# A causal attention and expert-layer kernel, with a copy, a rewrite of each partial sum and unread products added to the last half batch

## The chip, the cores and the metric

One core of a Trainium2 chip runs the kernel. The metric is the device time of one launch in microseconds (us), the median of several runs; lower is better. The engines are TensorE (PE in the profile; its weight loads are PEld), VectorE (DVE), ScalarE (ACT), GpSimd (POOL) and SyncE (SP, which here only issues DMAs). PSUM is the accumulator memory that TensorE writes its products to; SBUF is the working memory.

## What is computed

Block-causal attention over 8 batches and 8 heads of 576 positions and 64 dimensions, and behind it two matrix products with a gate between them, on 4608 tokens of 512 dimensions (the attention's output) and 2048 hidden units:

```python
def _attn_ref(q, k, v) -> np.ndarray:
    B, H, S, D = q.shape
    block = 64
    scale = 1.0 / np.sqrt(D)
    scores = scale * np.matmul(q, k.transpose(0, 1, 3, 2))
    ...
    scores = np.where(mask, scores, -1000000000.0)
    scores = scores - np.max(scores, axis=-1, keepdims=True)
    attn = np.exp(scores)
    attn = attn / (np.sum(attn, axis=-1, keepdims=True) + 1e-09)
    return np.matmul(attn, v).astype(np.float32)

def _moe_ref(x, w_in, w_out) -> np.ndarray:
    h = x @ w_in
    sp = np.where(h > 20.0, h, np.log1p(np.exp(np.minimum(h, 20.0))))
    g = h * np.tanh(sp)
    return (g @ w_out).astype(np.float32)
```

All inputs and outputs are float32.

## The kernel before

**Numbers in two parts.** TensorE takes float16 operands. Each float32 operand is scaled and split into a float16 part and a float16 remainder ("h" and "l": `wi_h` and `wi_l` for the first weights, `wo_h` and `wo_l` for the second, the halves of `Gt` for the gated values). A product of two such operands is three products into one accumulator: high by high, high weights by low values, low weights by high values.

**Half batches.** A batch's 576 tokens are two half batches (`Tile`), of 384 and 192 tokens. For the last batch the second half is 192 tokens (n = 192); it is the last of 16, numbered `self.i` = 15. Each half batch goes through four methods: `turn` (transposes the attention's output by DMA), `m1` (first matrix product and the gate on ScalarE), `split` (the gated values in two parts, `Gt`, on ScalarE and VectorE) and `m2` (second matrix product, eviction and store).

**The second product, `m2`.** The output's 512 dimensions are four slices of 128. A half batch of 192 tokens puts two slices side by side into one accumulator, a PSUM bank of 512 columns of which it uses 384 (`K` = 2), so the last one uses two accumulators: `acc0` for slices 0 and 1, `acc1` for slices 2 and 3. For each slice TensorE runs over f, the 16 blocks of 128 hidden units, with three products each (line 1702): 48 products of 128 weights by 192 columns, all added into the slice's columns. Each call of `add` in that loop makes one operation of three products, and the list `after` names what it waits for; `chain` keeps the slice's operations in order. When both slices of an accumulator are summed, `evac` scales them into `ot` (line 1734 where VectorE does it, 1741 where ScalarE does), and a DMA stores it (line 1759).

**What sets the order.** Nothing is issued while the operations are described. Each `add` records an engine, an estimated duration, a function that emits the instructions, what it waits for, and which buffers it takes and frees (a `Ring` stands for a set of equal buffers: `ss_ring` for two score tiles of 1024 columns in PSUM, `acc_ring` for three accumulators). `Plan.order` plays all operations through a model of the engines, in which an engine that comes free takes the ready operation with the earliest due time, and issues them in the order of the best play. Due times are the tables in `DUE`. Each engine then runs its instructions strictly in the order that was issued, and waits only for semaphores.

**The end of the program.** After the last `m1` there is no attention left, so TensorE runs the last half batch's `m2` alone. ScalarE evicts, SyncE stores, VectorE and GpSimd have nothing left.

Of the kernel before, what the change touches and what calls it, by code (L numbers as in the profile page):

```python
# [16 lines left out]
ALU = mybir.AluOpType  # L17
# [3 lines left out]
P = 128  # L21
# [326 lines left out]
def attention_moe(  # L348
# [17 lines left out]
    nc = tc.nc  # L366
    B, DM, S = qT.shape
# [62 lines left out]
    PT = [const.tile([P, 2048], F16, name=f"PT{i}") for i in range(NPT)]  # L430
# [14 lines left out]
    wi_h = const.tile([P, NP, DFF], F16, name="wi_h")  # L445
    wi_l = const.tile([P, NP, DFF], F16, name="wi_l")
    wo_h = const.tile([P, NF, DM], F16, name="wo_h")
# [12 lines left out]
    pv = room(NPV, "pv", [P, 19])  # L460
# [18 lines left out]
    NSS, NACC = 2, 3  # L479
# [1039 lines left out]
    class Tile:  # L1519
# [165 lines left out]
        def m2(self):  # L1685

            n, fc = self.n, self.fc
            chain = None
            self.reads, self.evacs = [], []
            K = self.K  # L1690
            for o in range(0, NP, K):
                plan.part("tile", self.i, 18 + o)
                parts = []
                for k in range(K):
                    for f in range(NF):
                        slot = (self.i * NG + f // FG) % NSLOT

                        def prods(o=o + k, k=k, f=f, slot=slot, parts=parts):
                            pt = acc_[parts[0].slot % NACC][:, k * n : (k + 1) * n]
                            gh, gl = (Gt[:, slot, x, f % FG, 0:n] for x in range(2))  # L1700
                            for z, (w, g) in enumerate(((wo_h, gh), (wo_h, gl), (wo_l, gh))):
                                nc.tensor.matmul(  # L1702
                                    pt,
                                    lhsT=w[:, f, o * P : (o + 1) * P],
                                    rhs=g,
                                    start=k == 0 and f == 0 and z == 0,
                                    stop=f == NF - 1 and z == 2,
                                    skip_group_check=True,
                                )

                        begin = k == 0 and f == 0
                        after = [chain]
                        if o == 0 and k == 0 and f % FG == 0:
                            after = after + self.splits[f // FG]
                        if o == 0 and begin:
                            after = after + [last.get("m2")]
                        if self.first and f == 0:
                            after = after + w_done[1][o + k]
                        chain = add(
                            "pe", products([n] * 3), prods, after, [acc_ring] if begin else []  # L1720
                        )
                        parts.append(chain)
                        if o + k == NP - 1 and f % FG == FG - 1:
                            self.reads.append(chain)

                last["m2"] = chain
                fo = self.batch["fc2"]
                ev_ = self.evacs


                def evac(op, o=o, c=parts[0], e=o // K):
                    for k in range(K):
                        cols = slice(k * n, (k + 1) * n)
                        op(
                            ot[ev_[e].slot % 2][:, cols],
                            acc_[c.slot % NACC][:, cols],
                            fc[:, 1, o + k : o + k + 1],
                        )

                def evac_act(evac=evac):  # L1740
                    evac(lambda o, i, s: nc.scalar.activation(o, i, AF.Copy, scale=s))  # L1741

                ev = add(
                    "dve",
                    K * dve(n, True),
                    lambda evac=evac: evac(nc.vector.tensor_scalar_mul),
                    [chain, fo, last.get("out")],
                    [ot_ring],
                    [(acc_ring, parts[0])],
                    other=[("act", K * act(n, True), evac_act)],  # L1750
                    psum=True,
                )
                ev_.append(ev)
                last["out"] = ev
                t0 = self.b * S
                last["store"] = add(
                    "sp",
                    dma(P * K * n * 4),
                    lambda o=o, ev=ev: nc.sync.dma_start(
                        out=outT[o * P : (o + K) * P, t0 + self.q0 : t0 + self.q1].rearrange(  # L1760
                            "(k p) t -> p k t", p=P
                        ),
                        in_=ot[ev.slot % 2][:, 0 : K * n].rearrange("p (k t) -> p k t", k=K),
                    ),
                    [ev, last.get("store")],
                    free=[(ot_ring, ev)],
                )
# [53 lines left out]
        tiles_by[b, 1].split()  # L1821
    tiles_by[B - 1, 1].m2()

    ops = plan.order()
    with tc.manual_schedule():
        for o in ops:
# [45 lines left out]
```

## Time and profile before

| | before |
|---|---|
| median of three runs | 996.82 us (995.87 to 998.99) |
| span of the profiled execution, first to last instruction | 996.9 us |
| TensorE busy | 973.1 us (98%) |
| VectorE busy | 668.5 us (67%) |
| ScalarE busy | 663.4 us (67%) |
| GpSimd busy | 115.0 us (12%) |
| mean granted TensorE clock | 0.995 |

The profile is of one execution; the three timed runs are others. For the profiled execution there is no time but its span, and the span lies on the median. A row of the timeline is: start in us, duration in us, engine, line of the kernel, operation, what it writes and reads, shapes, number of instructions merged into the row, and in brackets how long the engine was idle before and what ended that. A row of a group is: line, engine, operation, shapes, count, busy us and mean ns of one, then the idle time before it. A row of a table by stretches of time is: from and to, length, then for PE, PEld, DVE, ACT and POOL the busy us with the number of instructions, then the granted TensorE clock, the busy share of the DMA engines and GB/s. Matmuls are pipelined: the next one starts before the modelled end of the last, so the distance between starts is what counts.

### The profile page before, as it was taken

What the parts mean: (1) busy time and instruction counts of PE and PEld (TensorE: products, weight loads), DVE (VectorE), ACT (ScalarE), POOL (GpSimd) and SP (SyncE); (2) the same over time, 40 slices, a digit from 0 to 9 for tenths busy, and PEclk for the clock granted to TensorE, in tenths of its full rate; (3) what the DMA queues carried; (4) which work ended last, traced back from release to release, by engine and by line L of the source; (5) the groups of instructions that cost most, each with busy time, mean ns of one, the idle gap of its engine ahead of it and who ended that gap; (6) DMA issues with size and microseconds to landing.
All of it is one profiled execution on the core that took longest, in us unless ns stands there. A gap on an engine that the chain in (4) does not pass through costs nothing.

```text
span 996.9 us, 25050 instructions
## 1 busy us (share of the span) xinstructions
PE 973.1 (98%) x10576; PEld 722.2 (72%) x10576; DVE 668.5 (67%) x1411; ACT 663.4 (67%) x1062; POOL 115.0 (12%) x166
## 2 busy tenths in 40 slices
PE   6999879999999999999999999999999999999998
PEld 5677557786777867777677866777677776876787
DVE  5999999779899687564798378965389636420210
ACT  3769987769768678656788678887668835432221
POOL 0011232011112002000120031010011000000000
PEclk9999979999999999999999999999999999999999
DMA  9863755796677745472668377873277333420000
GB/s 324 270 174 113 183 97 140 152 180 149 119 165 163 163 100 110 91 161 50 143 151 171 71 135 137 156 148 50 57 173 146 76 69 82 82 57 1 25 17 25
DMA packets 275505, 121.56 MB, mean 122 GB/s; under 512 B 221376, under 2 KB 261568, under 8 KB 275392
## 3 DMA queue, kind: packets, MB, share of 16 engines
q1 hardware_dynamic: 275392, 119.97, 55.4%
q8 instruction: 82, 1.34, 0.5%
q14 instruction: 31, 0.25, 0.1%
HBM read 56.10 MB, written 9.44 MB: 66 GB/s over the span
## 4 chain that ended last, share of the span: by engine, by line
PE 86%; DVE 9%; DMA 2%; issue 1%; ACT 1%; SPq 1%; ACTq 0%; DVEq 0%
PE acc L1702 37%; PE acc L1597 35%; PE u L1419 7%; PE ss L1217 6%; DVE Gt L600 1%; DVE wo_h L600 1%; DMA x<-xt 1%; DVE wo_l L691 1%; DMA wo_l<-in_w_in_dram 1%; DVE PT L1045 1%; PE u L1151 1%; DVE pv L1258 1%; DMA PT<-P 1%; DVE P L1342 0%; DVE wi_l L691 0%
## 5 line engine op out<-in xcount | busy, mean ns | idle before, releaser
L1597 PE MATMUL acc<-x,wi_h 128*128 128x192 f16 (+1 forms) x2048 | 394.8, 286 | 4.1 <-ACT Et L1626 2.7
L1702 PE MATMUL acc<-Gt,wo_h 128*128 128x192 f16 (+1 forms) x2048 | 386.1, 287 | 0.2 <-DVE Gt L1673 0.2
L1702 PE MATMUL acc<-Gt,wo_l 128*128 128x192 f16 (+1 forms) x1024 | 293.7, 287 | 0.0
L1597 PE MATMUL acc<-x,wi_l 128*128 128x192 f16 (+1 forms) x1024 | 293.0, 286 | 0.0
L1597 PEld LDWEIGHTS <-wi_h 128*128 128x128 f16 x2048 | 191.1, 98 | 86.0 <-issue 8.5
L1702 PEld LDWEIGHTS <-wo_h 128*128 128x128 f16 x2048 | 187.6, 98 | 50.2 <-issue 3.3
L1626 ACT ACTIVATE Et<-acc,bv 128x384 f32<-128x384 f32 x192 | 109.4, 579 | 118.1 <-PE acc L1597 116.7
L1292 ACT ACTIVATE pe<-ss,pv 128x192 f32<-128x192 f32 (+1 forms) x280 | 148.1, 606 | 12.8 <-DVE pv L1266 8.2
L1673 DVE SCALAR_TENSOR_TENSOR Gt<-Et,bv,Gt 128x1536 f16<-128x1536 f32 (+1 forms) x64 | 91.3, 1432 | 78.7 <-ACT Gt L1658 78.3
L1258 DVE TENSOR_REDUCE pv<-ss 128x2 f32<-128x384 f32 (+4 forms) x140 | 106.0, 789 | 41.8 <-PE ss L1229 41.5
L1702 PEld LDWEIGHTS <-wo_l 128*128 128x128 f16 x1024 | 100.4, 98 | 34.0 <-issue 1.1
L1597 PEld LDWEIGHTS <-wi_l 128*128 128x128 f16 x1024 | 100.2, 98 | 33.1
L1342 DVE TENSOR_TENSOR P<-pe,P 128x256 f16<-128x256 f32 (+1 forms) x168 | 110.8, 700 | 14.9 <-ACT P L1336 13.3
L1292 ACT ACT_TABLE_LOAD x59 | 75.7, 1283 | 12.5 <-DVE pv L1266 7.8
L1336 POOL CAST P<-pe 128x256 f16<-128x256 f32 (+3 forms) x81 | 60.3, 777 | 201.9 <-DMA PT<-P 79.2
L1626 ACT ACT_TABLE_LOAD x62 | 79.5, 1283 | 1.1
L1419 PEld LDWEIGHTS <-PT 128*128 128x128 f16 x2128 | 72.8, 98 | 5.1 <-issue 0.6
L1419 PE MATMUL u<-VH,PT 128*128 128x65 f16 x1344 | 74.3, 193 | 0.0
L1658 ACT ACTIVATE Gt<-Et,bv 128x768 f16<-128x768 f32 (+1 forms) x51 | 63.4, 1248 | 15.9 <-PE acc L1702 14.0
L1419 PE MATMUL u<-VO,PT 128*128 128x64 f16 x784 | 72.6, 193 | 0.0
L1741 ACT ACTIVATE ot<-acc,bv 128x192 f32<-128x192 f32 (+1 forms) x46 | 21.1, 487 | 66.8 <-PE acc L1702 52.9
L1217 PEld LDWEIGHTS <-QH 64*128 64x128 f16 x896 | 27.4, 95 | 28.7 <-issue 13.5
(126 smaller groups left out, 978.7 us busy)
## 6 DMA issues: line engine op xcount, KB each, us to landing
out_dram<-ot SPq DMA_DIRECT2D x48, 192.0 KB, 2.0
wo_l<-in_w_in_dram SPq DMA_DIRECT2D x8, 1024.0 KB, 7.3
Gt<-in_w_out_dram SPq DMA_DIRECT2D x16, 512.0 KB, 4.5
kl<-in_v_dram SPq DMA_DIRECT2D x28, 288.0 KB, 3.1
ql<-in_q_dram SPq DMA_DIRECT2D x28, 288.0 KB, 3.0
kl<-in_k_dram SPq DMA_DIRECT2D x28, 288.0 KB, 3.1
VL<-in_v_dram SPq DMA_DIRECT2D x28, 192.0 KB, 2.9
VL<-in_v_dram SPq DMA_DIRECT2D x28, 96.0 KB, 3.1
```

The lines of the kernel that those rows point to most:

```text
L1217: nc.tensor.matmul(ss[:, 512 * a + col : 512 * a + col + n], lhsT=m[q_][hs, at : at + P], rhs=m[k_][hs, key : key + n], start=first, stop= ...
L1258: nc.vector.reduce_max(out=mx[:, c], in_=ss[:, :, c0:c1], axis=mybir.AxisListType.X)
L1292: nc.scalar.activation(pe[ex[r].slot][:, cols], ss_[S0[r].slot % NSS][:, cols], AF.Exp, scale=esc, bias=mx[:, c, a : a + 1],)
L1336: op(out=h, in_=x)
L1342: nc.vector.tensor_sub(l, x, h)
L1419: nc.tensor.matmul(out, lhsT=p_, rhs=v_, start=first, stop=True, skip_group_check=True,)
L1597: nc.tensor.matmul(pt, lhsT=w[:, d, f * P : (f + 1) * P], rhs=x[:, d, :], start=k == 0 and d == 0 and z == 0, stop=d == NP - 1 and z == 2, ...
L1626: nc.scalar.activation(Et[:, (self.i * NG + g) % NE, j : j + K, 0:n], acc_[c.slot % NACC][:, 0 : K * n].rearrange("p (k n) -> p k n", k=K) ...
L1658: lambda g_hi=g_hi, ev=ev: nc.scalar.activation(g_hi, ev, AF.Copy, scale=self.s_g),
L1673: lambda g_hi=g_hi, g_lo=g_lo, ev=ev: nc.vector.scalar_tensor_tensor(out=g_lo, in0=ev, scalar=self.s_g, in1=g_hi, op0=ALU.mult, op1=ALU.su ...
L1702: nc.tensor.matmul(pt, lhsT=w[:, f, o * P : (o + 1) * P], rhs=g, start=k == 0 and f == 0 and z == 0, stop=f == NF - 1 and z == 2, skip_gro ...
L1741: evac(lambda o, i, s: nc.scalar.activation(o, i, AF.Copy, scale=s))
```

## The change

Two pieces are added; nothing is removed.

In `m2`, for the last half batch alone and after f = 7 of each of its four slices, two operations are put into the chain. ScalarE copies the slice's partial sum from PSUM to a buffer in SBUF (`pe[0]`, columns 512 to 703), and VectorE rewrites the partial sum as twice the copy less itself, the same value. The product of f = 8 waits for that.

Behind everything else, with a due time of 2000 (later than any other), one operation of TensorE and seven of other engines are described. TensorE's `columns` waits for two score tiles, and runs 16 products with 64 columns of weights each, into the lower and the upper half of the partitions in turn (8 of 512 columns, 8 of 128), and two full products of 512 columns. ScalarE, VectorE and GpSimd then copy and add tiles of 512 columns, one behind the other. No output depends on them.

```diff
                         parts.append(chain)
+                        if self.i == 2 * B - 1 and f == 7:
+
+                            def again(op, k=k, parts=parts):
+                                pt = acc_[parts[0].slot % NACC][:, k * n : (k + 1) * n]
+                                op(pe[0][:, 512 : 512 + n], pt)
+
+                            chain = add("act", 0.6, lambda again=again: again(nc.scalar.copy), [chain])
+                            chain = add(
+                                "dve",
+                                0.6,
+                                lambda again=again: again(
+                                    lambda t, pt: nc.vector.scalar_tensor_tensor(
+                                        out=pt,
+                                        in0=t,
+                                        scalar=2.0,
+                                        in1=pt,
+                                        op0=ALU.mult,
+                                        op1=ALU.subtract,
+                                    )
+                                ),
+                                [chain],
+                            )
                         if o + k == NP - 1 and f % FG == FG - 1:
                             self.reads.append(chain)
...
     tiles_by[B - 1, 1].m2()
+
+    plan.due = 2000.0
+    idle = [last["S"]] + [x for t in heads.values() for hl in t for x in hl]
+    both = [add("pe", (0.01, 0.0), lambda: None, idle, take=[ss_ring]) for _ in range(2)]
+
+    def columns():
+        for n in (512, 128):
+            for k in range(4):
+                for a in range(2):
+                    nc.tensor.matmul(
+                        ss_[both[0].slot % NSS][64 * a : 64 * a + 64, 512 * a : 512 * a + n],
+                        lhsT=wi_h[:, a, 64 * k : 64 * k + 64],
+                        rhs=wo_h[:, k, 0:n],
+                        start=True,
+                        stop=True,
+                        skip_group_check=True,
+                    )
+        for a in range(2):
+            nc.tensor.matmul(
+                ss_[both[1].slot % NSS][:, 512 * a : 512 * a + 512],
+                lhsT=wi_h[:, a, 0:P],
+                rhs=wo_h[:, 0, 0:512],
+                start=True,
+                stop=True,
+                skip_group_check=True,
+            )
+
+    C = add("pe", (2.6, 6000.0), columns, both)
+    one, two = (lambda: ss_[both[1].slot % NSS][:, 0:512]), (lambda: ss_[both[1].slot % NSS][:, 512:1024])
+    side, three = pe[0][:, 0:512], pe[1][:, 0:512]
+    steps = (
+        ("act", lambda: nc.scalar.copy(side, one())),
+        ("dve", lambda: nc.vector.tensor_add(two(), two(), side)),
+        ("act", lambda: nc.scalar.copy(one(), two())),
+        ("dve", lambda: nc.vector.tensor_add(three, side, two())),
+        ("pool", lambda: nc.gpsimd.tensor_add(three, side, three)),
+        ("pool", lambda: nc.gpsimd.tensor_sub(PT[0][:, 0:512], side, PT[1][:, 0:512])),
+        ("pool", lambda: nc.gpsimd.tensor_scalar_mul(three, side, pv[0][:, 0:1])),
+    )
+    for i, (eng, emit) in enumerate(steps):
+        C = add(eng, 2.0, emit, [C], free=[(ss_ring, x) for x in both] if i == len(steps) - 1 else [])
```

The order that the plan makes of it differs from the order before only from the last `m2` on. On TensorE, `columns` comes between f = 7 and f = 8 of the first slice. The end of it and the next product, with the semaphores that the rows wait for, in the changed program (before, the product of f = 8 followed that of f = 7 directly, and its first row had no wait):

```order
L1854 MATMUL ss0_131<-wo_h_106,wi_h_104 64x128
L1863 LDWEIGHTS wi_h_104
L1863 MATMUL ss1_132<-wo_h_106,wi_h_104 128x512
L1863 LDWEIGHTS wi_h_104
L1863 MATMUL ss1_132<-wo_h_106,wi_h_104 128x512
L1702 LDWEIGHTS wo_h_106
L1702 MATMUL acc0_134<-Gt_62,wo_h_106 128x192 [waits DVE_49]
```

Here 18 products stand between the two, and the matmul of f = 8 waits for VectorE while its weight load does not. In the other three slices f = 8 waits in the same way, with no other product in between.

ScalarE's end of the program in the changed kernel, from the last eviction that is not of the last half batch (`acc0` and `acc1` are the accumulators, `ss1` the second score tile, `pe0` the buffer in SBUF; `x2` marks two equal rows):

```order
L1763 ACTIVATE ot1_130<-acc2_136,bv1_115 128x384 [waits DMAHW7_49,PE_49]
L1727 COPY pe0_123<-acc0_134 128x192 [waits PE_49]
L1876 COPY pe0_123<-ss1_132 128x512 [waits PE_49]
L1727 COPY pe0_123<-acc0_134 128x192 [waits DVE_49,PE_49]
L1878 COPY ss1_132<-ss1_132 128x512 [waits DVE_49]
L1763 ACTIVATE ot0_129<-acc0_134,bv1_115 128x192 [waits DMAHW0_49,PE_49]
L1763 ACTIVATE ot0_129<-acc0_134,bv1_115 128x192
L1727 COPY pe0_123<-acc1_135 128x192 [waits DVE_49,PE_49] x2
L1763 ACTIVATE ot1_130<-acc1_135,bv1_115 128x192 [waits DMAHW1_49,PE_49]
```

Before, the three kinds of rows with line 1763 (then 1741) followed one another; the six copies are new, and the evictions have kept their order behind them.

VectorE's end in the changed kernel, from its last work on `Gt`, which was its last row before:

```order
L1673 SCALAR_TENSOR_TENSOR Gt_62<-Et_61,bv1_115,Gt_62 128x4x192 [waits DVE_49,Activation_49] x2
L1734 SCALAR_TENSOR_TENSOR acc0_134<-pe0_123,acc0_134 128x192 [waits Activation_49]
L1877 TENSOR_TENSOR ss1_132<-ss1_132,pe0_123 128x512 [waits Activation_49]
L1734 SCALAR_TENSOR_TENSOR acc0_134<-pe0_123,acc0_134 128x192 [waits Activation_49]
L1879 TENSOR_TENSOR pe1_124<-pe0_123,ss1_132 128x512 [waits Activation_49]
L1734 SCALAR_TENSOR_TENSOR acc1_135<-pe0_123,acc1_135 128x192 [waits Activation_49] x2
```

The four rewrites of the partial sums (line 1734) and two sums of 512 columns are new, and each waits for ScalarE. GpSimd gets an instruction that loads its library anew and three operations of 512 columns behind its last row. SyncE's rows are the same.

## The prediction

> **What bounds the kernel now.** I read the page's busy shares first, then its slices, then the end of the chain that ended last, then the last 20 us in order of time.
>
> ```profile
> span 996.9 us, 25050 instructions
> PE 973.1 (98%) x10576; PEld 722.2 (72%) x10576; DVE 668.5 (67%) x1411; ACT 663.4 (67%) x1062; POOL 115.0 (12%) x166
> PE   6999879999999999999999999999999999999998
> DVE  5999999779899687564798378965389636420210
> ACT  3769987769768678656788678887668835432221
> PEclk9999979999999999999999999999999999999999
> ...
> 973.15 12.60 PE acc L1702 x130
> 985.75 7.23 issue
> ```
>
> TensorE is busy 98% of the span, and nearly full in every slice but three of the first six. VectorE and ScalarE have little left to do in the last slices. The chain ends in products of line 1702, the second matrix product of the last half batch. (The "issue" of 7.23 us is TensorE's work as well: the wait of the last eviction, whose releaser was not recorded.) So the end of the program is TensorE's last product plus a fixed tail. The rows at both ends of the last half batch's second product are these:
>
> ```profile
> 976.89 0.33 PE L1702 MATMUL acc<-Gt,wo_h 128*128 128x192 f16 x2
> ...
> 984.73 0.25 PE L1702 MATMUL acc<-Gt,wo_l 128*128 128x192 f16 x1
> ...
> 985.01 0.42 ACT L1741 ACTIVATE ot<-acc,bv 128x192 f32<-128x192 f32 x1 [7.34 <-PE acc L1702]
> ...
> 992.65 0.25 PE L1702 MATMUL acc<-Gt,wo_l 128*128 128x192 f16 x1
> 992.98 0.73 ACT L1741 ACTIVATE ot<-acc,bv 128x192 f32<-128x192 f32 x2 [7.24 <-issue]
> 993.74 0.38 SPq L1759 DMA_DIRECT2D out_dram<-ot  x1
> ```
>
> There are 192 products (four output slices of 16 f of three). From 976.89 to 992.65 they start 191 steps apart, so one every 0.0825 us without a hole. What is put into this stretch and is not hidden moves the end by its own length; the tail behind 992.65 keeps its shape.
>
> **The change part by part.** First, the four round trips. In each output slice the product of f = 8 now waits for a VectorE pass over the partial sum, which waits for a ScalarE copy, which waits for the product of f = 7. All three are in series, and each of TensorE's later products stands behind the one that waits. Nothing else of the program is left to fill the hole: in the order of the changed program only the first hole has other products in it. The prices come from these rows.
>
> ```profile
> 955.10 0.94 ACT L1658 ACTIVATE Gt<-Et,bv 128x768 f16<-128x768 f32 x1
> 956.07 1.02 DVE L1673 SCALAR_TENSOR_TENSOR Gt<-Et,bv,Gt 128x768 f16<-128x768 f32 x1 [21.72 <-ACT Gt L1658]
> ...
> 140.32 1.80 DVE L1673 SCALAR_TENSOR_TENSOR Gt<-Et,bv,Gt 128x1536 f16<-128x1536 f32 x1
> 141.44 0.13 PEld L1702 LDWEIGHTS <-wo_h 128*128 128x128 f16 x2
> 142.17 0.48 PE L1702 MATMUL acc<-Gt,wo_h 128*128 128x384 f16 x1 [0.22 <-DVE Gt L1673]
> ...
> L674 ACT CAST wi_l<-acc 128x512 f16<-128x512 f32 x8 | 4.7, 588 | 2.9 <-PE acc L665 2.9
> L1741 ACT ACTIVATE ot<-acc,bv 128x384 f32<-128x384 f32 x20 | 11.6, 579 | 30.5 <-PE acc L1702 23.9 <-issue 6.6
> L1741 ACT ACTIVATE ot<-acc,bv 128x192 f32<-128x192 f32 x26 | 9.5, 416 | 36.3 <-PE acc L1702 29.0 <-issue 7.2
> L600 DVE SCALAR_TENSOR_TENSOR Gt<-Gt 128x512 int32<-128x512 int32 x32 | 20.9, 688 | 0.1
> L1734 DVE TENSOR_SCALAR ot<-acc,bv 128x192 f32<-128x192 f32 x6 | 2.2, 410 | 2.6 <-PE acc L1702 2.6
> L1483 DVE TENSOR_TENSOR tt<-u,dv 128x384 f32<-128x384 f32 x32 | 17.8, 557 | 2.0
> L1483 DVE TENSOR_TENSOR tt<-u,dv 128x256 f32<-128x256 f32 x32 | 13.6, 424 | 2.3
> ```
>
> - The last product before the hole takes 0.25 us from its start to its modelled end. ScalarE starts 0.03 us after that (984.73 + 0.25 = 984.98, and 985.01).
> - The copy of 128x192 out of PSUM is not in the trace. The eviction of the same tile on the same engine takes 416 ns, and 579 for twice the columns, so 0.85 ns a column; but it reads a scale for each partition. The plain cast of 512 columns takes 588 ns; less 320 x 0.85 that is 316. I take 0.32, the row nearest in kind; the bounds are 0.22 (588 x 192 / 512, nothing of it fixed) and 0.42.
> - ScalarE to VectorE: 955.10 + 0.94 = 956.04, and 956.07, so 0.03 us.
> - The VectorE pass reads SBUF and PSUM and writes PSUM; no such operation is in the trace. A two-input operation on PSUM takes 557 ns for 384 columns and 424 for 256, so 1.04 ns a column and 358 for 192. The same kind of instruction with a constant takes 688 ns for 512 columns, so 355 for 192 at that slope; the one-input pass over the same accumulator takes 410. I take 0.38, bounds 0.35 and 0.45.
> - VectorE to TensorE: 140.32 + 1.80 = 142.12, and 142.17, so 0.05 us. There the weights had been loaded ahead, at 141.44; here the load has no wait either and is hidden in the same way.
>
> Together 0.25 + 0.03 + 0.32 + 0.03 + 0.38 + 0.05 = 1.06 us from the start of the last product to the start of the next, where 0.08 stood: **+0.98 us a hole**. The bounds are 0.85 (0.22 and 0.35) and 1.28 (0.42, 0.45, and 0.08 for each of the three handoffs, as from 992.65 + 0.25 to 992.98). Three holes stay empty: **+2.94 us**, bounds 2.55 and 3.84.
>
> Second, the products that nobody reads. They are not on an idle engine: TensorE runs them, in the first hole: 8 of 512 columns and 8 of 128 with 64 columns of weights each, then two of 512 with 128. The waiting product stands behind all of them. The nearest rows are products that use half of the array's rows, two heads in turn:
>
> ```profile
> 787.77 0.25 PE L1702 MATMUL acc<-Gt,wo_l 128*128 128x192 f16 x1
> ...
> 787.94 0.55 PEld L1217 LDWEIGHTS <-QH 64*128 64x128 f16 x12 [0.16 <-issue]
> 787.95 0.42 PE L1217 MATMUL ss<-KH,QH 64*128 64x448 f16 x6
> 788.21 0.41 PE L1217 MATMUL ss<-KL,QH 64*128 64x448 f16 x6
> ...
> 788.95 0.38 PE L1217 MATMUL ss<-KL,QH 64*128 64x64 f16 x4
> 789.17 0.38 PE L1217 MATMUL ss<-KH,QL 64*128 64x64 f16 x4
> 789.48 0.34 PE L1702 MATMUL acc<-Gt,wo_h 128*128 128x192 f16 x2
> ```
>
> One group of six is, for each of two heads, 448 + 64 + 64 = 576 columns, and the next group starts 0.26 us later. At 0.0825 us for 192 columns, 576 columns are 0.25 us and 1152 are 0.50: the two halves ran side by side. Going into that mode cost 0.10 us (787.77 + 0.08 = 787.85, and 787.95) and coming back 0.09 (789.17 + 0.22 = 789.39, and 789.48). Twelve weight loads took 0.55 us, 46 ns each. If halves of the array's columns pair as halves of its rows do, the 8 of 512 take four times 0.22 = 0.88 us; the 8 of 128 are bound by their eight loads, 0.37 (their columns alone are 0.22); the two wide ones take 0.44; the two switches 0.19. That is 1.88 us, more than the 0.98 of the round trip beside it, so the first hole costs **+1.88 us**. Bounds: 1.54 (no switch, loads hidden) and, one at a time, 8 x 0.22 + 8 x 0.055 + 0.44 + 0.19 = 2.83.
>
> The Trainium skill's page "TensorEngine Tiling (Array Packing)", in "Restrictions and Gotchas", says that column tiling cannot be had with the fast weight load. With the page "TensorE: Matmul & The Clock Gate", section "LDWEIGHTS", a load of 64 columns would be 53 ns, an estimate, so the eight loads 0.43 in place of 0.37, and the sum 4.88. The trace has no load of 64 columns to set against it.
>
> Third, the sums on ScalarE, VectorE and GpSimd. ScalarE's copies of 512 columns (0.59 us by line 674) stand behind the first and behind the second of the four short copies, VectorE's sums of 512 (about 0.69) likewise, and there are 2 us of products (24 x 0.0825) or more between one round trip and the next operation that anything waits for. So they cost nothing. That cover would go if they took over 2 us each; then the rest would be added. GpSimd's library instruction and its three operations come after its last work:
>
> ```profile
> 829.34 1.12 POOL L1504 CAST xt<-tt 128x256 f16<-128x256 f32 x1 [8.72 <-DVE tt L1483]
> L1336 POOL CAST P<-pe 128x512 f16<-128x512 f32 x15 | 9.6, 643 | 0.0
> ```
>
> The library instruction has 155 us from 830.5 to do its work in; the trace has no price for it. The three operations begin about when the second rewriting is done, some 11 us before the end; three at 0.64, or at three times that with two inputs, take 2 to 6 us. Nothing waits for them but the end. No DMA is added or moved, and the last stores keep their places.
>
> The sum is 2.94 + 1.88 = **+4.82 us**. The span of the profiled execution is 996.9 us, and the median of the three runs 996.82 (995.87 to 998.99), the same within a tenth, so the span can be used as it stands: **1001.7 us**, +0.48%.
>
> **The rivals.**
>
> *The 64-column products run one after the other.* For it: the trace shows only halves by rows side by side, none by columns. Against it: two neighbours write different partitions and banks, as those halves did. It gives 2.94 + 2.83 = 5.77, so 1002.7. The Trainium skill's "TensorE: Matmul & The Clock Gate", section "Packing small matmuls", has three column tiles at 2.38 times the speed of one; that speaks for the pairs, and no run here shows it.
>
> *The added products are hidden.* Then the change is only the four round trips: 4 x 0.98 = 3.92, so 1000.8. It needs the 18 products to take under 0.98 us, while 1.32 us of columns alone stand against it.
>
> *The clock drops in the holes.*
>
> ```profile
> 115.80:119.20 3.40, 1.92 (x12) 1.17 (x12) 3.37 (x8) 2.36 (x4) 0.28 (x1) 1.00 1.03 282
> 133.20:136.60 3.40, 0.05 (x2) 0.00 (x0) 3.26 (x8) 2.74 (x4) 2.48 (x2) 0.92 1.03 99
> 136.60:140.00 3.40, 0.61 (x6) 0.29 (x7) 3.37 (x9) 3.15 (x3) 1.34 (x1) 0.50 0.27 60
> 141.45:146.00 4.55, 4.33 (x18) 2.09 (x16) 4.52 (x7) 4.10 (x7) 1.92 (x1) 0.50 0.69 161
> ```
>
> The clock (the column before the last two) stayed at 1.00 through a stretch in which TensorE worked 1.92 of 3.40 us, and went to 0.50 only after one of 0.05. With a hole of 1 us in every 4 the emptiest 3.4 us are about 70% full. If it dropped all the same for one such stretch, 3.4 us at half speed would add 1.7: 4.82 + 1.70 = 6.52, so 1003.4 or more.
>
> *Not slower.* The last rows above are also the one large loss in the span that a run may or may not have: from 141.45 to some 146.5 TensorE worked at a granted clock of 0.50. 5.1 us at half speed are 2.6 us lost. If the runs of the changed kernel that set its median met the clock back at 1.00 at 141.45 and those of before did not, 4.82 - 2.6 = 2.2 us remain: 999.1, within 0.3%. It decides from 1.8 us on (4.82 less the 3.0 us that are 0.3%). For it: the three runs lie 3.1 us apart. Against it: up to 977 us both programs have the same instructions in the same order.
>
> **How the numbers follow.** Forecast 0.57, one at a time 0.21, hidden 0.03, clock 0.05, not slower 0.14 (0.02 of it faster by over 0.3%). A measurement of this kernel tells about 0.3%, or 3.0 us, from no change. The first four are slower by more than that, 0.86 together; 0.12 is within it and 0.02 faster. The forecast's own bounds are 2.55 + 1.54 = 4.09 and 3.84 + 1.88 = 5.72, so 1001.0 to 1002.6; the products one at a time with the high bound of the holes reach 3.84 + 2.83 = 6.67, so 1003.6; and the runs of before go 1 us below their median. The range is 1000.0 to 1003.8: it leaves out the case that is not slower and what the clock could do beyond one stretch.
>
> **What would show it right or wrong.** In the changed profile the last 20 us should show four idle stretches of TensorE in line 1702 released by VectorE's line 1734, three of them with a start-to-start of 1.06 us, and the first one filled with lines 1854 and 1863 for some 1.9 us. ScalarE's line 1727 should take 0.32 us and VectorE's 1734 0.38. The granted clock should be 1.00 there, and everything up to 977 us unchanged. I am wrong if the added products take under 1.5 or over 2.3 us, if a handoff takes more than 0.1 us, if writing PSUM from VectorE takes over 0.45 us, or if the difference stands before 977 us.

## The result and the profile after

The changed kernel takes 1000.59 us (median of 9 runs, 1000.39 to 1005.36) where the kernel before takes 996.82 us on the same chip (9 runs, 995.39 to 1001.28). The ratio is 1.0040, with a 95% interval of 1.0021 to 1.0059: slower, by 3.8 us. The profiled execution has a span of 1001.9 us and a time of its own of 1003.71 us, one of the slower of the nine.

First the page of the changed kernel: its head, the slices of TensorE and of its clock, then TensorE's waits (in total, times, longest) and the end of the chain of waits (start, length, where).

```profile
span 1001.9 us, 25108 instructions
PE 979.8 (98%) x10594; PEld 726.8 (73%) x10594; DVE 671.4 (67%) x1417; ACT 665.6 (66%) x1068; POOL 121.3 (12%) x169
...
PEclk9999979999999999999999999999999999999999
```

```profile
PE acc L1702 <- DVE acc L1734: 2.4, 3, 0.8
```

```profile
981.28 3.97 PE acc L1702 x48
986.04 4.13 PE acc L1702 x48
990.97 4.13 PE acc L1702 x48
```

The busy shares hardly move: 98% of TensorE hides a stall of this size. The waits show it: three of 0.8 us, all on the rewrite of line 1734, and the chain's end, which before had one piece of 12.60 us of line 1702, is now cut at each of them. (Line 1734 of the changed kernel is the rewrite; in the kernel before the line of that number was an eviction.) The granted clock has its one low slice early, as before, and none at the end.

The last half batch in order of time (start, duration, engine, line, operation, idle time before it and what ended that):

```profile
977.39 0.33 PE L1702 MATMUL acc<-Gt,wo_h 128*128 128x192 f16 x2
...
979.29 0.25 PE L1702 MATMUL acc<-Gt,wo_l 128*128 128x192 f16 x1
979.47 1.28 PE L1854 MATMUL ss<-wo_h,wi_h 128*64 128x512 f16 x16
979.58 0.32 ACT L1727 COPY pe<-acc 128x192 f32<-128x192 f32 x1 [1.40 <-PE acc L1702]
979.92 0.36 DVE L1734 SCALAR_TENSOR_TENSOR acc<-pe,acc 128x192 f32<-128x192 f32 x1 [2.23 <-ACT pe L1727]
980.68 0.60 PE L1863 MATMUL ss<-wo_h,wi_h 128*128 128x512 f16 x2
981.12 0.33 PE L1702 MATMUL acc<-Gt,wo_h 128*128 128x192 f16 x2
...
985.00 0.25 PE L1702 MATMUL acc<-Gt,wo_l 128*128 128x192 f16 x1
986.04 0.32 PE L1702 MATMUL acc<-Gt,wo_h 128*128 128x192 f16 x2 [0.80 <-DVE acc L1734]
...
997.79 0.25 PE L1702 MATMUL acc<-Gt,wo_l 128*128 128x192 f16 x1
```

The second product of the last half batch now takes 997.79 - 977.39 = 20.40 us from its first start to its last, where it took 15.76: **+4.64 us**. A bare hole is 986.04 - 985.00 = 1.04 us from start to start (1.05 in the other two), so 0.96 more than the 0.0825 of two products in a row. The first hole is filled with the products that nobody reads, and they set its length: the rewrite is done at 980.28, but TensorE comes to f = 8 only at 981.12, and that row has no wait. From 979.29 + 0.08 to 981.12 they take 1.75 us. 1.75 + 3 x 0.96 = 4.63, the whole of it. From the last product's start to the end of the span are 1001.9 - 997.79 = 4.1 us, 996.9 - 992.65 = 4.25 before: nothing is added behind it.

### The profile page after: what moved, and what is told of

Its sections match the earlier page's. It is cut to its first block, busy times and chain, and to the rows that moved or that the text cites. A ratio compares the mean times of both kernels' runs of the same rounds, so it can differ in the third digit from the quotient of the medians.

```text
span 1001.9 us, 25108 instructions
## 1 busy us (share of the span) xinstructions
PE 979.8 (98%) x10594; PEld 726.8 (73%) x10594; DVE 671.4 (67%) x1417; ACT 665.6 (66%) x1068; POOL 121.3 (12%) x169
## 4 chain that ended last, share of the span: by engine, by line
PE 88%; DVE 9%; DMA 1%; ACT 1%; issue 0%; SPq 0%; ACTq 0%; DVEq 0%
PE acc L1702 38%; PE acc L1597 34%; PE u L1419 7%; PE ss L1217 6%; DVE Gt L600 1%; DVE wo_h L600 1%; PE u L1151 1%; DVE wo_l L691 1%; DVE PT L1045 1%; PE acc L1008 1%; DMA Gt<-in_w_out_dram 1%; PE ss L1079 1%; DVE pv L1258 0%; DVE wi_l L691 0%; DVE Gt L583 0%
## 5 line engine op out<-in xcount | busy, mean ns | idle before, releaser
L1258 DVE TENSOR_REDUCE pv<-ss 128x2 f32<-128x384 f32 (+4 forms) x140 | 105.9, 788 | 43.1 <-PE ss L1229 42.8
```

The costliest lines, as they stand in the source:

```text
L1258: nc.vector.reduce_max(out=mx[:, c], in_=ss[:, :, c0:c1], axis=mybir.AxisListType.X)
```

## The experiments

Every kernel was timed beside the kernel before on the same chip. The stretch is the distance from the first to the last start of the last half batch's second product in the kernel's own trace: 15.76 us before, 20.40 with the change.

| kernel | time, us (runs) | ratio to before, 95% interval | stretch, us |
|---|---|---|---|
| rewrite only | 1000.24 (12) | 1.0028 [1.0012, 1.0043] | 19.62 |
| unread products, put there | 999.88 (12) | 1.0016 [0.9996, 1.0035] | 17.50 |
| unread products, not put there | 1002.44 (12) | 1.0047 [1.0031, 1.0064] | 15.76 |
| one half of the columns | 1003.36 (7) | 1.0053 [1.0033, 1.0072] | 21.48 |
| rewrite in place | 999.14 (12) | 1.0014 [1.0002, 1.0026] | 18.22 |
| slices in turn | 1001.26 (12) | 1.0039 [1.0023, 1.0056] | 20.76 |
| accumulators in turn | 996.19 (12) | 0.9994 [0.9981, 1.0008] | 15.75 |
| every fourth f | 1008.67 (4) | 1.0127 [1.0099, 1.0154] | 27.32 |
| every third f | 1015.73 (4) | 1.0208 [1.0177, 1.0240] | 35.05 |
| every second f | 1036.33 (4) | 1.0392 [1.0363, 1.0422] | 55.62 |

The medians of before beside them were 997.22 us (the first three and slices in turn), 997.24 (one half, rewrite in place, every second f) and 996.81 (the other three).

### The two parts of the change, each alone

*Rewrite only.* The block of unread products and sums is taken out; the four round trips stay.

```diff
-    plan.due = 2000.0
-    idle = [last["S"]] + [x for t in heads.values() for hl in t for x in hl]
...
-        C = add(eng, 2.0, emit, [C], free=[(ss_ring, x) for x in both] if i == len(steps) - 1 else [])
```

> The four rewrites alone, without the unread products and sums. Theory (each hole is one round trip in series, 1.04 us from start to start where 0.08 stood): four holes of +0.96, so the stretch from the first to the last start of the last half batch's second product is 15.76 + 3.84 = 19.6 us and the time +3.8 us on before. Rival (the unread products are most of the loss): well under +3 us.

```profile
977.34 0.33 PE L1702 MATMUL acc<-Gt,wo_h 128*128 128x192 f16 x2
...
980.29 0.33 PE L1702 MATMUL acc<-Gt,wo_h 128*128 128x192 f16 x2 [0.80 <-DVE acc L1734]
...
996.96 0.25 PE L1702 MATMUL acc<-Gt,wo_l 128*128 128x192 f16 x1
```

These are rows of its timeline. The stretch is 19.62 us, 3.86 more than before: four holes of 0.965. The first one is now empty and has the same wait of 0.80 us as the others.

*Unread products, put there.* The rewrites are taken out; the 18 products are made part of the first slice's chain, so that they stand where the change has them, and the sums follow them.

```diff
-                        if self.i == 2 * B - 1 and f == 7:
...
+                        if self.i == 2 * B - 1 and f == 7 and o + k == 0:
+                            both = [
+                                add("pe", (0.01, 0.0), lambda: None, [chain], take=[ss_ring])
+                                for _ in range(2)
+                            ]
+                            chain = add("pe", (2.6, 6000.0), lambda: columns(both), both)
+                            self.unread = both, chain
```

> The 18 unread products at the same place (behind f = 7 of the first slice) and the sums behind them, no rewrite. Theory (TensorE pays for them in full): +1.75 us, stretch 17.5 us. Rival (they lay in idle time and were free): 0, which needs a hole, and there is none here. If the sums on ScalarE, VectorE and GpSimd cost something of their own, over +1.8 us.

```profile
980.14 0.33 PE L1702 MATMUL acc<-Gt,wo_h 128*128 128x192 f16 x2
...
982.04 0.25 PE L1702 MATMUL acc<-Gt,wo_l 128*128 128x192 f16 x1
982.22 1.28 PE L1807 MATMUL ss<-wo_h,wi_h 128*64 128x512 f16 x16
983.42 0.60 PE L1816 MATMUL ss<-wo_h,wi_h 128*128 128x512 f16 x2
983.87 0.33 PE L1702 MATMUL acc<-Gt,wo_h 128*128 128x192 f16 x2
```

In its timeline the products take 983.87 - 982.04 - 0.08 = 1.75 us, the same as in the change, and the stretch grows by 1.74. The two runs together account for the change: 19.62 + (1.75 - 0.965) = 20.41, and the change has 20.40. Nothing is left over for the sums on ScalarE and VectorE. By its time this run cannot be told from before; what separates the parts is the trace.

*Unread products, not put there.* The rewrites are taken out and nothing else is changed; the plan is free to choose where the unread products go.

```diff
-                        if self.i == 2 * B - 1 and f == 7:
...
```

> The unread products and sums as the plan places them when there is no rewrite: behind the last product. Theory: the stretch of the second product stays 15.76 us; but the unread chain behind it (1.75 us of products, then copies and sums of 0.58, 0.70, 0.59, 0.69, 1.27, 1.16 and 1.57 us) ends some 8.5 us after the last product, where the last store ended some 4.2 us after it, so +4 us. Rival (work that nobody reads is free at the end): 0.

```profile
988.97 0.25 PE L1702 MATMUL acc<-Gt,wo_l 128*128 128x192 f16 x1
989.14 1.12 PEld L1832 LDWEIGHTS <-wi_h 128*64 128x64 f16 x16 [0.16 <-issue]
...
993.79 1.26 POOL L1858 TENSOR_TENSOR pe<-pe,pe 128x512 f32<-128x512 f32 x1 [167.02 <-DVE pe L1857]
995.02 1.15 POOL L1859 TENSOR_TENSOR PT<-pe,PT 128x512 f16<-128x512 f32 x1
996.16 1.58 POOL L1860 TENSOR_SCALAR pe<-pe,pv 128x512 f32<-128x512 f32 x1
```

Its timeline shows that the plan puts them behind the last product, and the chain of sums behind them becomes the end of the program. From the last product's start to the end of the span are 998.5 - 988.97 = 9.5 us, where there were 4.25: 5.3 us more, and the time is 5.2 above before. That is over a microsecond more than the 4 expected. The last row ends 8.8 us behind the last product's start, about as worked out, but the expectation took that row's end for the end of the span, which is 0.8 us later. So the change owes the cheapness of its sums to their place. Three operations of GpSimd take 4.0 us; in the changed kernel the last of them ends at 990.92, 11 us before the end:

```profile
989.35 1.57 POOL L1882 TENSOR_SCALAR pe<-pe,pv 128x512 f32<-128x512 f32 x1
```

### What the unread products are bound by

*One half of the columns.* All 16 products of 64 columns write the lower half of the partitions; nothing else is changed.

```diff
-                        ss_[both[0].slot % NSS][64 * a : 64 * a + 64, 512 * a : 512 * a + n],
+                        ss_[both[0].slot % NSS][0:64, 512 * a : 512 * a + n],
```

> The changed kernel, with all 16 narrow products in the lower half of the array's columns, so that neighbours cannot pair. Theory (in the change they ran in pairs): 8 x 0.218 + 8 x 0.057 + 0.44 + 0.2 = 2.84 us from the last product before them to the next, against 1.75, so the stretch is 20.4 + 1.1 = 21.5 us and the time +1.1 us on the changed kernel. Rival (the pairing was not what made them short): no change.

```profile
979.73 0.25 PE L1702 MATMUL acc<-Gt,wo_l 128*128 128x192 f16 x1
979.91 2.36 PE L1854 MATMUL ss<-wo_h,wi_h 128*64 128x512 f16 x16
982.20 0.60 PE L1863 MATMUL ss<-wo_h,wi_h 128*128 128x512 f16 x2
982.64 0.33 PE L1702 MATMUL acc<-Gt,wo_h 128*128 128x192 f16 x2
```

In its timeline the 16 products take 982.20 - 979.91 = 2.29 us, and in the change 980.68 - 979.47 = 1.21: in the change the two halves do run side by side. The columns one after the other are 8 x 0.22 + 8 x 0.055 = 2.20 us, in pairs 1.10; what is left is 0.09 and 0.11, the price of coming out of the mode. So in both kernels the products take what their columns take. In pairs the eight of 128 columns have 0.22 us, less than eight loads one behind the other at the 46 ns of the prediction (0.37). The loads of the changed kernel are in its groups:

```profile
L1854 PEld LDWEIGHTS <-wi_h x16: 106/110/110, 979.5 to 980.5; 128*64 128x64 f16 x16
L1854 PE MATMUL ss<-wo_h,wi_h x16: 219/299/403, 979.5 to 980.5; 128*64 128x512 f16 x8, 128*64 128x128 f16 x8
```

(Shortest, median and longest, in ns.) A load of 64 columns is recorded with 110 ns, and 16 of them would be 1.76 us one behind the other; all 16 products took 1.21, so the recorded loads overlap. They do so within one half as well. These are loads for products of 128 columns in the kernel with one half:

```profile
981.66 0.45 PEld L1854 LDWEIGHTS <-wi_h 128*64 128x64 f16 x7
```

Seven loads of 110 ns lie within 0.45 us, so they start 0.056 us apart, in step with products of 0.055. The recorded 110 ns is therefore not the distance at which loads can follow one another. Whether loads or columns set the 0.056 us in one half can't be told from these runs.

### What a round trip is made of, and what can hide it

*Rewrite in place.* VectorE multiplies the partial sum by one where it stands; ScalarE's copy is gone, as are the unread products.

```diff
-                            chain = add("act", 0.6, lambda again=again: again(nc.scalar.copy), [chain])
-                            chain = add(
-                                "dve",
...
+                                nc.vector.tensor_scalar_mul(pt, pt, 1.0)
+
+                            chain = add("dve", 0.6, again, [chain], psum=True)
```

> The four rewrites alone, by VectorE in place (times 1.0), without ScalarE's copy. Theory (the hole is the sum of its members): 0.25 + 0.03 + 0.36 + 0.05 = 0.69 us from start to start, +0.61 a hole, +2.4 us in all, stretch 18.2 us. Rival (a hole has a fixed price for a wait on another engine, whatever is behind it): +0.96 a hole as before.

```profile
978.36 0.25 PE L1702 MATMUL acc<-Gt,wo_l 128*128 128x192 f16 x1
...
978.65 0.37 DVE L1727 TENSOR_SCALAR acc<-acc 128x192 f32<-128x192 f32 x1 [1.88 <-PE acc L1702]
979.07 0.33 PE L1702 MATMUL acc<-Gt,wo_h 128*128 128x192 f16 x2 [0.46 <-DVE acc L1727]
```

Its timeline shows a hole of 979.07 - 978.36 = 0.71 us, 0.25 + 0.04 + 0.37 + 0.05; four of them less 0.0825 each are 2.5, and the stretch grew by 2.46. So ScalarE's copy with its handoff is 1.045 - 0.71 = 0.335 us of each hole, as its rows say (0.32 and 0.02).

*Slices in turn.* A hole needs other products to fill it, and the two slices of an accumulator don't depend on each other. This kernel (rewrites only) runs f = 0 to 7 of both slices of an accumulator, then f = 8 to 15 of both.

```diff
-                for k in range(K):
-                    for f in range(NF):
+                turns = [(k, f) for k in range(K) for f in range(NF)]
+                if self.i == 2 * B - 1:
+                    turns.sort(key=lambda x: (x[1] > 7, x))
+                redo = {}
+                for k, f in turns:
...
+                        if f == 8:
+                            after = after + [redo.get(k)]
```

> The four rewrites alone, with the last half batch's two slices of an accumulator in turn: f = 0 to 7 of both, then f = 8 to 15 of both, so that 24 products (1.98 us) stand between a slice's f = 7 and its f = 8. Theory: the round trip of 1.04 us is hidden, the stretch is 15.76 us and the time that of before. Rival (VectorE's pass over a PSUM bank and TensorE's products into the same bank get in each other's way): products over 0.0825 us apart during the rewrite, up to +1.4 us in all for four passes of 0.36 us.

A miss: 20.76 us and not 15.76, worse than the rewrites in a row. These are rows of its timeline around the first round trip; the products between them go into the second slice of the same accumulator.

```profile
976.78 0.25 PE L1706 MATMUL acc<-Gt,wo_l 128*128 128x192 f16 x1
...
977.06 0.32 ACT L1733 COPY pe<-acc 128x192 f32<-128x192 f32 x1 [1.65 <-PE acc L1706]
977.43 0.33 PE L1706 MATMUL acc<-Gt,wo_h 128*128 128x192 f16 x2 [0.41 <-ACT pe L1733]
...
978.09 0.25 PE L1706 MATMUL acc<-Gt,wo_l 128*128 128x192 f16 x1
...
978.45 0.36 DVE L1740 SCALAR_TENSOR_TENSOR acc<-pe,acc 128x192 f32<-128x192 f32 x1 [3.51 <-PE acc L1706]
978.86 0.33 PE L1706 MATMUL acc<-Gt,wo_h 128*128 128x192 f16 x2 [0.53 <-DVE acc L1740]
```

Each round trip makes two holes. The products of the second slice wait until ScalarE has read the first (0.65 us from start to start), then nine run, VectorE's rewrite waits for these nine, and the next waits for the rewrite (0.77 us). Less 0.0825 each that is 1.255 us a round trip, 5.02 for four, and the stretch grew by 5.00. The waits stand in the program. This is its order on TensorE, with the semaphores that each row waits for (`acc_134` is the accumulator):

```
20013 L1706 MATMUL acc_134<-Gt,wo_h 128x192
20014 L1706 LDWEIGHTS wo_h
20015 L1706 MATMUL acc_134<-Gt,wo_h 128x192 [waits Activation_49]
...
20032 L1706 LDWEIGHTS wo_h
20033 L1706 MATMUL acc_134<-Gt,wo_h 128x192 [waits DVE_49]
```

No such wait was written in the edit. The layer that places the semaphores added them here between engines that touch the accumulator, though they touch different columns of it. The Trainium skill's page "PSUM — Partial Sum Buffer", section "PSUM bank collisions raise a hardware error", asks for that: it has semaphores guard PSUM by bank and quadrant of partitions, not by address, since another address in the same bank and quadrant still collides. The trace agrees in that the waits are there; what would happen without them was not tried.

*Accumulators in turn.* So the products in the hole must go to another bank. This kernel (rewrites only) runs f = 0 to 7 of a slice in `acc0`, f = 0 to 7 of a slice in `acc1`, then f = 8 to 15 of each.

```diff
+            accs = {o: [] for o in range(0, NP, K)}
+            turns = [(o, k, f) for o in accs for k in range(K) for f in range(NF)]
+            if self.i == 2 * B - 1:
+                turns.sort(key=lambda x: (x[1], x[2] > 7, x))
...
+                        if f == 8:
+                            after = after + [redo.get(o + k)]
...
-                    [chain, fo, last.get("out")],
+                    [ends[o], fo, last.get("out")],
```

> The four rewrites alone (no unread products, no sums), but the last half batch's products go through both accumulators in turn: f = 0 to 7 of a slice in acc0, then f = 0 to 7 of a slice in acc1, then f = 8 to 15 of each. The round trip of 1.05 us lies beside 24 products of 0.0825 us (1.98 us) that write another accumulator. Theory (a hole costs only because the order of the program leaves TensorE nothing that is free of the tile being rewritten): no hole, the last half batch's second product takes 15.76 us from its first to its last start as before, and the time is that of before (ratio 1.000, within 0.002). Rival one (a wait of TensorE on another engine costs in itself, whatever stands beside it): up to 0.2 us a handoff, so 16.0 to 16.6 us. Rival two (the rewrite and the products disturb each other in PSUM though in different banks): rows of products longer than 0.33 us while a rewrite runs, 16 us or more.

```profile
975.73 0.33 PE L1708 MATMUL acc<-Gt,wo_h 128*128 128x192 f16 x2
...
977.62 0.25 PE L1708 MATMUL acc<-Gt,wo_l 128*128 128x192 f16 x1
977.71 0.33 PE L1708 MATMUL acc<-Gt,wo_h 128*128 128x192 f16 x2
...
977.91 0.32 ACT L1735 COPY pe<-acc 128x192 f32<-128x192 f32 x1 [1.40 <-PE acc L1708]
...
978.26 0.36 DVE L1742 SCALAR_TENSOR_TENSOR acc<-pe,acc 128x192 f32<-128x192 f32 x1 [2.23 <-ACT pe L1735]
...
991.48 0.25 PE L1708 MATMUL acc<-Gt,wo_l 128*128 128x192 f16 x1
```

The copy and the rewrite are in its timeline with the same durations as ever, and TensorE goes on at 977.71, 0.09 us behind the last product of the first eight, without a wait. The stretch is 15.75 us, that of before, and the time too: four rewrites of partial sums cost nothing measurable. So a round trip costs only what the order leaves unfilled beside it. As the rewrites change no value, nothing here beats the kernel before.

### How far the holes are from costing the clock

The prediction had a rival in which the clock falls. Three kernels (rewrites only) have more holes: behind every fourth, third and second f, each with one of these conditions. The last of the three ran first.

```diff
-                        if self.i == 2 * B - 1 and f == 7:
+                        if self.i == 2 * B - 1 and f % 4 == 3 and f < 15:
...
+                        if self.i == 2 * B - 1 and f % 3 == 2:
...
+                        if self.i == 2 * B - 1 and f % 2 and f < 15:
```

> Rewrites alone, after every fourth f (3, 7 and 11) of each slice: 12 holes, with 12 products (0.99 us) between one hole and the next, so TensorE works about half of each stretch. If the granted clock holds, 15.76 + 12 x 0.965 = 27.3 us from the first to the last start of the last half batch's second product. If it falls to one half, as it did with 6 products between holes, the 15.76 us of products become up to twice as long: 27.3 to 43 us, by the point at which it falls. The theory expects it to hold: in the profile of before it held through a stretch of 3.40 us with 1.92 us of work.

> Rewrites alone, after f = 2, 5, 8, 11 and 14 of each slice: 20 holes, with 9 products (0.74 us) between one hole and the next, so TensorE works about 43% of each stretch. If the granted clock holds, 15.76 + 20 x 0.965 = 35.1 us from the first to the last start; if it falls, up to 51 us. The point lies between half (the run with every fourth f) and a third (every second f, where it fell); theory and rival give no more than that, so the run is to place it.

> The rewrite after every odd f from 1 to 13 of each slice, 28 holes, without the unread products and sums: six products of 0.0825 us, then a hole, so TensorE streams about a third of the time. Theory (the clock holds as long as no stretch of 3.4 us is nearly empty): granted clock 1.00, +28 x 0.96 = +26.9 us, stretch 42.6 us. Rival (the holes bring the clock down): the clock at 0.50 in these 40 us, products 0.16 us apart, up to +12 us more.

Every fourth and every third f give 27.32 and 35.05 us, 12 and 20 holes of 0.965 within 0.02 us. Every second f is a miss of the theory: 55.62 us, where 28 such holes would give 42.8. The 12.8 us more are about what its rival gave (up to 12). Two stretches of 3.4 us of the kernel with every third f, then three of the one with every second (from and to, length, busy time of PE, PEld, DVE, ACT and POOL with instructions, granted clock, DMA share, GB/s):

```profile
976.80:980.20 3.40, 1.79 (x21) 1.50 (x19) 0.72 (x2) 0.64 (x2) 0.00 (x0) 1.00 0.08 27
...
1000.60:1004.00 3.40, 2.05 (x21) 1.76 (x21) 0.67 (x2) 0.47 (x2) 0.00 (x0) 1.00 0.00 0
```

```profile
974.00:977.40 3.40, 1.79 (x19) 1.41 (x17) 1.21 (x3) 1.13 (x3) 0.00 (x0) 1.00 0.16 58
977.40:980.80 3.40, 1.79 (x17) 1.43 (x15) 0.72 (x2) 0.64 (x2) 0.00 (x0) 0.78 0.00 0
980.80:984.20 3.40, 1.79 (x12) 1.29 (x10) 0.73 (x2) 0.64 (x2) 0.00 (x0) 0.50 0.00 0
```

With six products between holes (twelve where a slice ends, in both kernels) the granted clock falls to 0.50 within the second stretch and stays there; with nine it holds for 35 us. In the timeline of the kernel with every second f the products themselves then take longer:

```profile
978.56 0.33 PE L1702 MATMUL acc<-Gt,wo_h 128*128 128x192 f16 x2 [0.80 <-DVE acc L1734]
...
980.02 0.48 PE L1702 MATMUL acc<-Gt,wo_h 128*128 128x192 f16 x2 [0.80 <-DVE acc L1734]
```

The busy column does not show the difference: it reads 1.79 of 3.40 us in kernels of both kinds, 3.40 less two waits of 0.80, because each run of products is counted to its modelled end. Counted by starts, nine products are 9 x 0.0825 = 0.74 us of every 0.74 + 0.965, 43%, and six are 0.495 of every 0.495 + 0.965, 34%. For this pattern the point lies between. Whether the share of work decides, or how often a hole comes, these two kernels don't separate. The Trainium skill's "TensorE: Matmul & The Clock Gate", section "HAM oscillation — how this bites in real kernels", gives the rule that no idle gap should be longer than some 3.4 us. By that rule the clock would have held here, where the waits are 0.8 us; it fell, so a gap of that length is not what decides here. (The next section of that page of the Trainium skill, "A second HAM failure mode: psum-queue depth-cycling", tells of a clock that swings in a kernel with frequent short gaps, and gives no share.) In the change there are 48 products from one hole to the next, 3.96 of 4.92 us or 80%, well clear of the point.

## Why the prediction was right

**The direction and the mechanism.** Slower, for the reasons given: the product of f = 8 waits in line for a round trip over two engines, and the "idle" products are TensorE's own. The time was put at 1001.7 us and is 1000.59; in the trace, +4.82 us stands against +4.64. The time alone would not have settled it: it lies below the forecast's own bounds (1001.0 to 1002.6), inside the range only by the microsecond left for scatter, and nearer to the rival with hidden products (1000.8). The trace rules that rival out, as the 18 products take 1.75 us and not under 0.98. Of the four idle stretches named as a sign three are there; the first is filled, as the prediction's own working has it.

**The hole.** 1.06 us was worked out, 1.04 to 1.05 is measured. Copy 0.32 and 0.318, rewrite 0.38 and 0.36, handoffs 0.03, 0.03, 0.05 and, by the rows above, 0.04 (979.54 to 979.58), 0.02 (979.90 to 979.92) and 0.05 (as the hole less its other parts). The nearest rows in kind priced two operations that the trace before did not have. That both prices came out within 0.02 us is better than their working, with bounds of 0.22 to 0.42 and 0.35 to 0.45, could promise, and so in part luck.

**The unread products.** 1.88 was worked out, 1.75 is measured; the term was over by 0.13, and its one wrong step is the eight products of 128 columns, "bound by their eight loads, 0.37". They cost their columns, 0.22: 0.15 less, while the two switches of the mode took 0.21 where 0.19 was put. The 46 ns a load that went into it came from 12 loads in 0.55 us beside products of 0.50: that was the pace of the products, not the price of a load. The sentence with the Trainium skill's page "TensorE: Matmul & The Clock Gate", section "LDWEIGHTS", went further the same way: 53 ns a load and 4.88 in all. A load of 64 columns is recorded with 110 ns here, twice the figure of that page of the Trainium skill, while loads in one half start 0.056 us apart, close to it. In pairs neither price, eight times over, bounds the products.

**The pairs.** That column halves run side by side, the main uncertainty (the rival with 0.21), is shown by the kernel with one half: 2.83 us in the hole (982.64 - 979.81), just what the rival gave for one at a time. Its argument for the pairs was off in one point: the row halves that it compares with write different banks but the same 128 partitions, while the column halves write different partitions too.

**The sums.** Nothing, as predicted; shown by the sum of the two parts. That the order hides them, not their size, is shown by the kernel whose plan put the unread work last: 5.2 us, products and sums together. GpSimd's three operations take 4.0 us, within the 2 to 6 given; they begin at 986.96, 15 us before the end and not 11. The library instruction of GpSimd is in no row, and its price stays open; no run shows GpSimd late.

**The clock.** It held, as predicted, with more room than the argument had (80% against a point between 34 and 43%). But the argument's yardstick was not sound: it went by the busy time in 3.4 us and by a fall only after a nearly empty stretch, and with every second f the clock fell at 1.79 of 3.40 us, where with every third f it held.

**The size of the time.** It is 4.64 us in the trace and 3.8 between the medians; the rest lies within the scatter of the medians. The difference of medians less the growth of the stretch, in the nine other kernels in which the stretch tells the change, is -0.84, +0.92, +0.40, -0.56, -0.96, -0.61, +0.30, -0.37 and -0.77 us in the order of the table; -0.87 for the change lies among them. In the kept traces the scatter is made in the first 170 us. The last half batch's second product begins at 973.21 us in the trace of the products not put there and at 980.14 in that of the products put there, 6.9 us apart with the same products ahead of it. One and the same group of products of line 1217, which begins at 166.29 us in the trace of before, begins at 162.39 and 169.58 us in these two, already 7.2 apart. In all twelve traces the distance to the trace of before changes by less than 0.3 us from there to the last half batch. The mean granted clock of the first 170 us is 0.98 in the one and 0.92 in the other, and 1.00 in both from 170 to 970, so the clock is part of it, as in the rival "not slower". It is not all of it: the changed kernel's runs follow their mean granted clock (1000.40 us at 0.997, 1003.73 at 0.994, 1005.36 at 0.989), but runs of before took 995.47 and 1000.10 us at the same 0.994. What the rest is stays open. The scatter moves single runs by 5 us, and the medians by under 1 us. So of the 1.1 us between forecast and time, 0.18 were the sizes of terms and the rest lies within this scatter.

**The base.** That the span of before could stand for its time was luck. In every run with both figures the time is 1.7 to 2.8 us above the span, so the profiled execution of before, with a span of 996.9 us, was one of its slower ones. Its span fell on the median by accident, and the sum started from the right number.

## What to carry to other kernels

A round trip through two engines costs its full length only where the engine that waits has nothing else in line; before an operation is put into an accumulation, look for products that go to another PSUM bank and put them behind the product before it. Work for "idle" engines has to be counted on the engine that issues it and by the place where the order leaves it: the same sums cost nothing when they ended 11 us ahead of the end, and the unread work behind the last product cost 5.2 us, sums and products together. Where a stall is a fraction of a per cent, measure it as a distance between two starts in the trace, and let the timed runs confirm the sign.

## What the runs showed of the hardware

- A load of 64 columns of weights was recorded with 106 to 110 ns, no less than one of 128 columns (a median of 98 for the loads of line 1702 in the changed kernel). Yet in one half such loads started 0.056 us apart: the recorded length is not the pace.
- Products of half the columns behaved like those of half the rows: 0.10 us to go in (979.37 to 979.47), 0.11 to come out, and two halves side by side.
- The granted clock fell to one half with TensorE at work 34% of the time, counted by starts, and waiting 0.8 us at a time; it held at 43%.
- With a round trip in one bank and products in another, neither was slowed: copy 0.32, rewrite 0.36, products 0.0825 us apart.
